# Bucketed attention with a rational feed-forward: the row maxima are clamped behind their transpose, and the bucket rows are scaled on ACT

## The chip, the cores and the metric

One core of a Trainium2 chip. Its engines are PE (TensorE: matmuls, with PEld, its weight loads, beside it), DVE (VectorE), ACT (ScalarE), POOL (GpSimd) and SP (SyncE, which issues most DMAs). Each engine works through its own queue in program order and waits on semaphores. The metric is the device time of one execution in microseconds (us); shorter is better.

## What is computed

Attention over 4 x 8 heads of 768 tokens and 64 dimensions, in which a query sees only the keys of its own hash bucket (6 bits, the signs of a projection), then a feed-forward layer whose activation is a quotient of polynomials:

```python
q_bits = (np.einsum('bhsd,dk->bhsk', q, proj) > 0).astype(np.int64)
...
mask = q_bucket[:, :, :, None] == k_bucket[:, :, None, :]
scores = scale * np.matmul(q, k.transpose(0, 1, 3, 2))
scores = np.where(mask, scores, -1000000000.0)
scores = scores - np.max(scores, axis=-1, keepdims=True)
attn = np.exp(scores)
attn = attn / (np.sum(attn, axis=-1, keepdims=True) + 1e-09)
out = np.matmul(attn, v)
...
P = a[0] + a[1] * h + a[2] * h2 + a[3] * h3          # h = x @ w_in
Q = 1.0 + np.abs(b[0]) * np.abs(h) + np.abs(b[1]) * h2
return (P / (Q + 1e-06)) @ w_out
```

## The kernel before

The heads are taken in 16 pairs (`p`), each in 12 steps (`s`): a step is one tile of 128 keys by 384 queries for both heads of the pair. What happens to a pair:

- `high`, `low`, `second_low`, `second_high`, `high_move` split q and k into a high and a low part and lay them out as matmul operands (Q1, K1, Q2, K2). The subtraction `low` writes a tile `lo` of which only one exists for q and one for k, so it waits until the DMAs of `second_low` have read the pair before.
- `bits` finds the bucket bits of two pairs at once (`psb`, 16 matmuls), turns them into signs on DVE, and scales the q rows by 2^60 (`mb`, a second DVE instruction). `maskrows` moves these rows by DMA into rows 64 to 76 of Q1 and K1, so that a matmul over 76 rows adds a huge negative number where the buckets differ.
- `maxstep` computes a 128-query strip of scores (`psm`, two buffers) and DVE reduces it to its row maximum, one column of `m`. Twelve such columns make a pair.
- `shift_clamp` clamps the maxima and changes their sign (`nm`, DVE, SBUF to SBUF). `shift_turn` transposes them on PE (`pst`, against the identity in `cst`) and copies the result out of PSUM (`mt`, ACT). `shift_rows` moves `mt` by DMA into row 76 of Q1: the scores then come out with the maximum taken off.
- `scores` computes the score tiles again (`pss`), ACT takes their exponential (`E`), and POOL adds the tiles up for the denominators (`acc`). `values` multiplies by v (`psv`). `pss` and `pst` share one PSUM tag of three buffers (`s`).

Pair p's `high`, `low`, `bits` and `maxstep` run during the two pairs before it, so in the steady state every step of a pair holds its own `scores` and `values` and a `maxstep` of the next pair or the one behind it. In between, `weights` converts the feed-forward weights, which arrive as 64-bit floats (`wr`, `ws`, `wi_lo`: some ACT and DVE instructions per block). Two pairs differ from two others only in that every second one holds a `bits`, and every fourth the reciprocals of a batch.

The order is written out by hand: `at(p, s, f, ...)` files a call under the number 12 p + s, and the plan is issued in the order of these numbers (equal ones in the order of filing). Every engine keeps this order. Pair 0 is special: its maxima come in two halves, each clamped, turned and stored by itself (`hf` 0 and 1), ahead of and during its own first steps.

The feed-forward part follows (`Ffn`: `psh`, `pso`), and shares no instruction with the functions named above.

Of the kernel before, what the change touches and what calls it, by code (L numbers as in the profile page):

```python
# [7 lines left out]
F32 = mybir.dt.float32  # L8
# [3 lines left out]
AF = mybir.ActivationFunctionType  # L12
ALU = mybir.AluOpType
# [4 lines left out]
P = 128  # L18
S = 768
HQ = 384  # L20
NT = S // P
# [13 lines left out]
CLAMP = 2.0 ** 40  # L35
# [30 lines left out]
def move(nc, out, in_, queue=None):  # L66

    (queue or nc.sync).dma_start(out.bitcast(F32), in_.bitcast(F32))
# [3 lines left out]
def bucket_attention_then_rational_ffn(ctx, tc, qT, kT, v, proj, w_in, w_out, coef, consts, out):  # L72
# [55 lines left out]
    def operands_to_terms():  # L128
        early.close()
        ffn.terms_pool(right)  # L130

    last = attention(tc, nc, raw, ps_b, tail, tokens, early, operands_to_terms, ffn, load, QF, KF, v, w_in, w_out, wo_d, ident, cst,
                     ones, prj, wi_hi, wi_lo, x_d, s_d, r_d, coefficients)
    ffn.rest(ctx, last)
# [3 lines left out]
def attention(ctx, tc, nc, raw, ps_b, tail, tokens, early, operands_to_terms, ffn, load, QF, KF, v, w_in, w_out, wo_d, ident, cst, ones, prj,  # L138
# [9 lines left out]
    sm = ctx.enter_context(tc.tile_pool(name="sm", bufs=1))  # L148
# [5 lines left out]
    Q1, Q2, K1, K2, LO, V, M, MB, ACC, EXP, AV, MS = ({} for _ in range(12))  # L154

    def load_v(p, queue=nc.sync):
        V[p] = operand("v", p, [P, NT, P], F32)
        queue.dma_start(V[p], v[p])
# [3 lines left out]
    def high(p, t):  # L162
        F, T, n = ((QF, Q1, "q"), (KF, K1, "k"))[t]
        T[p] = operand(f"{n}1", p, [P, 2, S], F32R, 3)
        nc.scalar.copy(T[p][:, t, :], F[p])

    def high_move(p):
        for T, g in ((Q1[p], 0), (K1[p], 1)):
            move(nc, T[0:64, 1 - g, :], T[64:128, g, :])

    def low(p, t, engine=nc.vector):
        F, T = ((QF, Q1), (KF, K1))[t]
        LO[p, t] = raw.tile([P, S], F32R, tag=f"lo{t}", name=f"lo{t}_{p}", bufs=1)
        engine.tensor_tensor(out=LO[p, t], in0=F[p], in1=T[p][:, t, :].bitcast(F32), op=ALU.subtract)
# [13 lines left out]
    def bits(p, which=(0, 1)):  # L188

        if which[0] == 0:  # L190
            mb = sm.tile([P, 2, HQ], F32R, tag="mb", name=f"mb{p}")
            MB[p], MB[p + 1] = (mb, 0), (mb, 64)
        mb = MB[p + which[0]][0]
        sl = slice(64 * which[0], 64 * which[-1] + 64)
        ps = ps_a.tile([P, 2, 512], F32, tag="psa", name=f"psb{p}_{which[0]}")
        for hf in range(2):
            for w in which:
                for t, F in enumerate((QF[p + w], KF[p + w])):
                    o = 64 * w + 32 * t
                    nc.tensor.matmul(ps[o : o + 32, hf, 0:HQ], prj[:, t, :], F[:, hf * HQ : hf * HQ + HQ], start=True, stop=True)  # L200
        rows = mb[sl]
        nc.vector.tensor_scalar(out=rows, in0=ps[sl, :, 0:HQ], scalar1=0.0, scalar2=cst[sl, 0:1], op0=ALU.is_gt, op1=ALU.subtract)
        nc.vector.tensor_scalar(out=rows, in0=rows.bitcast(F32), scalar1=cst[sl, 1:2], scalar2=None, op0=ALU.mult)

    def maskrows(p, queues=(None, None)):
        mb, o = MB.pop(p)
        for h in range(2):
            o1 = o + 14 * h
            move(nc, Q1[p][64:76, h, :], mb[o1 : o1 + 12].rearrange("p f c -> p (f c)"), queues[0])
            move(nc, K1[p][64:77, h, :], mb[o1 + 32 : o1 + 45].rearrange("p f c -> p (f c)"), queues[1])  # L210
# [9 lines left out]
        nc.vector.tensor_reduce(out=M[p][:, j : j + 1], in_=ps[:, :, 0:HQ], axis=AX.XY, op=ALU.max)  # L220


    def shift_clamp(p, hf=None):
        m = M[p].rearrange("p (h f i) -> p h f i", h=2, f=2)
        m = m if hf is None else m[:, :, hf : hf + 1, :]
        n = NT if hf is not None else 2 * NT
        MS[p] = sm.tile([P, n], F32, tag="nm", name=f"nm{p}_{hf}")
        nc.vector.tensor_scalar(out=MS[p].rearrange("p (h f i) -> p h f i", h=2, i=NT // 2), in0=m, scalar1=-CLAMP, scalar2=-1.0,
                                op0=ALU.max, op1=ALU.mult)

    def shift_turn(p, hf=None):
        n = NT if hf is not None else 2 * NT
        ps = ps_b.tile([P, 512], F32, tag="s", bufs=3, name=f"pst{p}_{hf}")
        nc.tensor.transpose(ps[0:n, 0:P], MS.pop(p), ident)
        MS[p] = sm.tile([n, P], F32R, tag="mt", name=f"mt{p}_{hf}")
        nc.scalar.copy(MS[p], ps[0:n, 0:P])

    def shift_rows(p, hf=None):
        cs = slice(0, S) if hf is None else slice(hf * HQ, hf * HQ + HQ)
# [62 lines left out]
    def recips(bb):  # L302
        n = 2 * NHP * S // P
        s = tail.tile([P, n], F32, tag="rs", name=f"rs{bb}")
        nc.sync.dma_start(s, s_d[bb].rearrange("h (x c) -> (h x) c", c=n))
        yield
        z = tail.tile([P, n], F32, tag="rz", name=f"rz{bb}")
        d = tail.tile([P, n], F32, tag="rd", name=f"rd{bb}")
        r = tail.tile([P, n], F32, tag="rr", name=f"rr{bb}")
        nc.vector.tensor_scalar(out=z, in0=s, scalar1=0.0, scalar2=S * TINY, op0=ALU.is_equal, op1=ALU.mult)  # L310
        nc.vector.tensor_scalar(out=d, in0=s, scalar1=0.0, scalar2=1e-9, op0=ALU.is_gt, op1=ALU.mult)
        nc.vector.tensor_tensor(out=d, in0=s, in1=d, op=ALU.add)
        nc.vector.tensor_tensor(out=d, in0=d, in1=z, op=ALU.add)
        nc.vector.reciprocal(out=r, in_=d)
        yield
        nc.sync.dma_start(r_d[bb].rearrange("h (x c) -> (h x) c", c=n), r)
        yield
# [43 lines left out]
    def at(p, s, f, *args):  # L361
        plan.setdefault(12 * p + s, []).append((f, args))

    def spread(p, steps, gen):
        for s in steps:
            at(p, s, lambda g: next(g, None), gen)

    for p in range(NPAIR):
        for s in range(12):
            at(p, s, scores, p, s)  # L370

            if p > 1:
                at(p - 2, 7 + s if p > 2 else 9 + 0.85 * s, maxstep, p, s)

            if not 0 < p < NPAIR - 1:
                at(p, s + 2.3, values, p, s)
            elif s % 2:
                at(p, s + 1.3, values, p, s - 1)
                at(p, s + 1.3, values, p, s)
            if s % NT == NT - 1:  # L380
                at(p, s + (1.3 if 0 < p < NPAIR - 1 else 2.3), values_out, p, s // NT)
        for hf in range(2):
            at(p, 6 * hf + 9, values_store, p, hf)
        if p < NPAIR - 1:
            at(p, 14.5, sums, p)
            at(p, 16, sums_store, p)
        if p > 1:
            for t in range(2):
                at(p - 2, t, high, p, t)
                at(p - 2, 2 + t, low, p, t)  # L390
            if p % 2 == 0:
                at(p - 2, 3 if p == 2 else 2, bits, p)
            at(p - 2, 2, high_move, p)
            at(p - 2, 6 if p == 2 else 4, maskrows, p)
        if p > 0:
            at(p - 1, 0, second_low, p)
            at(p - 1, 3, second_high, p)
            at(p - 1, 4, load_v, p)
            d = 1.5 if p == 1 else 0
            at(p - 1, 7 + d, shift_clamp, p)  # L400
            at(p - 1, 8 + d, shift_turn, p)
            at(p - 1, 10 if d == 0 else 9.6, shift_rows, p)
        if p > 3:
            at(p - 4, 6, load, p)
        if p % NHP == NHP - 1 and p + 1 < NPAIR:
            spread(p, (20, 22, 23), recips(p // NHP))
# [12 lines left out]
    for t in range(2):  # L419
        high(0, t)  # L420
        low(0, t)
    bits(0, (0,))
    high_move(0)
    maskrows(0, (nc.sync, nc.scalar))
    load(2, nc.scalar)
    load_v(0, nc.scalar)
    bits(0, (1,))
    for t in range(2):
        high(1, t)
    second_low(0)  # L430
# [5 lines left out]
        at(-2, when[s], maxstep, 0, order[s])  # L436
        at(0, 0.6 + 0.7 * s, maxstep, 1, s)
    for hf in range(2):
        for s, f in ((5, shift_clamp), (6.5, shift_turn), (6.6, shift_rows)):
            at(-2, 19.5 * hf + s, f, 0, hf)  # L440
    for t in range(2):
        low(1, t, nc.gpsimd)
# [211 lines left out]
```

## Time and profile before

| | |
|---|---|
| median of 3 runs | 1029.55 us (1029.2 to 1035.9) |
| the profiled execution | 1029.27 us, of which the span from first to last instruction is 1027.5 |
| PE busy | 977.0 us (95%), 5009 matmuls |
| DVE busy | 907.9 us (88%) |
| ACT busy | 678.9 us (66%) |
| POOL busy | 384.8 us (37%) |
| mean granted clock of PE | 0.971 |

All rows of a trace name line 61, since a helper records every operation; instructions are told apart by their tiles (`out<-in`). Busy time is the union of an engine's instructions; a matmul's end is modelled, so a busy PE need not be PE at its peak. In rows in order of time the columns are start, length (both us), engine, operation, tiles, and in brackets the idle time of the engine before it and what ended it; neighbours that are alike are merged (xN). In rows of waits they are total us, times, longest. Groups give busy us and the mean ns of one.

### The profile page before, as it was taken

The numbers are of one execution on the slowest core, as the hardware profiler recorded it, in microseconds if no ns is written. First come the engines' busy times: TensorE is split into PE (matmuls) and PEld (weight loads), VectorE is DVE, ScalarE is ACT, GpSimd is POOL, SyncE is SP. The second block draws the span as 40 slices with busy tenths as digits, with TensorE's granted clock in tenths as the row PEclk, the third lists the DMA queues.
The fourth block names the chain that finished last, engine by engine and source line by source line (L and its number), as shares of the span: only waits on it lengthen the run. The fifth ranks groups of instructions, "written<-read, shape, count | busy, mean of one in ns | idle before, by whom it ended". The sixth has DMA issues, their size and how long they took to land.

```text
span 1027.5 us, 14486 instructions
## 1 busy us (share of the span) xinstructions
PE 977.0 (95%) x5009; PEld 749.4 (73%) x5009; DVE 907.9 (88%) x1207; ACT 678.9 (66%) x1419; POOL 384.8 (37%) x268
## 2 busy tenths in 40 slices
PE   6899988989898988999999999999999999999998
PEld 2565555555555555564999999999999999999996
DVE  5688788878978787767999999999999999999996
ACT  1466555656656655567877777777777777777775
POOL 1255554545545454556222222222222222222222
PEclk7799999999999999899999999999999999999999
DMA  7765564656656664673740201101111010020000
GB/s 202 195 165 175 165 177 124 177 163 186 187 165 211 206 205 134 177 217 118 283 137 15 69 11 62 32 1 62 32 57 36 1 62 31 1 72 22 32 1 31
DMA packets 50489, 112.95 MB, mean 110 GB/s; under 512 B 9296, under 2 KB 21968, under 8 KB 50416
## 3 DMA queue, kind: packets, MB, share of 16 engines
q1 hardware_dynamic: 49580, 110.59, 35.8%
q10 hardware_dynamic: 836, 1.44, 0.5%
q8 instruction: 39, 0.64, 0.3%
q14 instruction: 34, 0.28, 0.1%
HBM read 56.82 MB, written 21.17 MB: 76 GB/s over the span
## 4 chain that ended last, share of the span: by engine, by line
PE 78%; DVE 13%; DMA 3%; issue 2%; ACT 2%; SPq 1%; DVEq 0%; ACTq 0%
PE psh L61 26%; PE pso L61 26%; PE psv L61 10%; PE pss L61 9%; PE psm L61 4%; DVE m L61 3%; DVE wr L61 2%; DVE ws L61 2%; DVE nm_None L61 2%; PE psu L61 2%; DVE wi_lo L61 2%; ACT E L61 1%; DMA k<-k 1%; PE psb L61 1%; SPq L61 1%
## 5 line engine op out<-in xcount | busy, mean ns | idle before, releaser
L61 POOL TENSOR_TENSOR gl<-c,gh 128x384 fp32r<-128x384 f32 x128 | 140.6, 1099 | 396.0 <-ACT gh L61 369.4
L61 DVE TENSOR_REDUCE m<-psm 128x1 f32<-128x768 f32 x192 | 180.1, 949 | 76.8 <-PE psm L61 76.2
L61 PE MATMUL pso<-wo,gh 128*128 128x512 f32 x768 | 241.1, 395 | 0.0
L61 ACT ACTIVATE E<-pss 128x384 f32<-128x384 f32 x384 | 168.4, 490 | 97.9 <-PE pss L61 92.4
L61 POOL TENSOR_TENSOR acc<-E,E 128x768 f32<-128x768 f32 x64 | 126.2, 1972 | 190.3 <-ACT E L61 190.3
L61 PE MATMUL pss<-q,k 77*128 77x384 f32 (+1 forms) x768 | 183.1, 361 | 3.0 <-DMA q<-mt 2.6
L61 PEld LDWEIGHTS pss<-q,k 77*128 77x128 f32 (+1 forms) x768 | 136.7, 196 | 64.6 <-issue 54.4
L61 PE MATMUL psh<-xl,wi_hi 128*128 128x384 f32 x512 | 172.1, 336 | 0.0
L61 PE MATMUL psh<-xh,wi_hi 128*128 128x384 f32 x512 | 171.7, 335 | 0.0
L61 PE MATMUL psh<-xh,wi_lo 128*128 128x384 f32 x512 | 171.5, 335 | 0.0
L61 PEld LDWEIGHTS pso<-wo,gh 128*128 128x128 f32 x768 | 142.9, 188 | 23.7
L61 PE MATMUL psv<-E,v 128*64 128x385 f32 x768 | 157.3, 529 | 0.0
L61 PE MATMUL pso<-wo,gl 128*128 128x512 f32 x384 | 152.2, 396 | 0.3 <-POOL gl L61 0.3
L61 DVE SCALAR_TENSOR_TENSOR c<-c,ab,r 128x384 f32<-128x384 f32 x128 | 147.1, 1149 | 0.0
L61 ACT ACTIVATE h<-psh 128x384 f32<-128x384 f32 x128 | 63.1, 493 | 122.4 <-PE psh L61 122.4
L61 POOL TENSOR_TENSOR acc<-acc,E 128x768 f32<-128x768 f32 x64 | 113.9, 1780 | 30.1 <-ACT E L61 27.5
L61 PE MATMUL psm<-k,q 76*128 76x384 f32 x384 | 111.1, 374 | 13.9 <-DVE m L61 9.8
L61 PEld LDWEIGHTS psh<-xh,wi_hi 128*128 128x128 f32 x512 | 96.1, 188 | 6.3 <-issue 1.2
L61 PEld LDWEIGHTS psh<-xl,wi_hi 128*128 128x128 f32 x512 | 96.0, 188 | 5.1
L61 PEld LDWEIGHTS psh<-xh,wi_lo 128*128 128x128 f32 x512 | 96.1, 188 | 0.0
L61 PEld LDWEIGHTS psm<-k,q 76*128 76x128 f32 x384 | 71.7, 204 | 31.8 <-DVE m L61 22.2
L61 PEld LDWEIGHTS psv<-E,v 128*64 128x64 f32 x768 | 47.6, 141 | 64.1 <-issue 56.7
(63 smaller groups left out, 1322.6 us busy)
## 6 DMA issues: line engine op xcount, KB each, us to landing
q<-q SPq DMA_DIRECT2D x48, 192.0 KB
k<-k SPq DMA_DIRECT2D x48, 192.0 KB
wr<-w_in SPq DMA_DIRECT2D x16, 512.0 KB
wr<-w_out SPq DMA_DIRECT2D x16, 512.0 KB
wo_d<-wr SPq DMA_DIRECT2D x16, 512.0 KB
wo<-wo_d SPq DMA_DIRECT2D x16, 512.0 KB
q<-lo SPq DMA_DIRECT2D x32, 192.0 KB
k<-lo SPq DMA_DIRECT2D x32, 192.0 KB
```

The source lines that it names most:

```text
L61: return self.tc.keep_in_program_order(issue(*args, **kwargs))
```

## The change

The maxima are transposed as they stand; the clamp and the change of sign happen on DVE when the result is read out of PSUM, where ACT copied it before. For the two halves of pair 0, whose columns are not adjacent, DVE first copies six columns into a tile. The scaling of the bucket rows becomes a function of its own, `penalties`, on ACT, filed one step behind `bits`.

```diff
-        rows = mb[sl]
-        nc.vector.tensor_scalar(out=rows, in0=ps[sl, :, 0:HQ], scalar1=0.0, scalar2=cst[sl, 0:1], op0=ALU.is_gt, op1=ALU.subtract)
-        nc.vector.tensor_scalar(out=rows, in0=rows.bitcast(F32), scalar1=cst[sl, 1:2], scalar2=None, op0=ALU.mult)
+        nc.vector.tensor_scalar(out=mb[sl], in0=ps[sl, :, 0:HQ], scalar1=0.0, scalar2=cst[sl, 0:1], op0=ALU.is_gt, op1=ALU.subtract)
+
+    def penalties(p, which=(0, 1)):
+        sl = slice(64 * which[0], 64 * which[-1] + 64)
+        rows = MB[p + which[0]][0][sl]
+        nc.scalar.activation(rows, rows.bitcast(F32), AF.Identity, scale=cst[sl, 1:2])
...
-    def shift_clamp(p, hf=None):
-        m = M[p].rearrange("p (h f i) -> p h f i", h=2, f=2)
-        m = m if hf is None else m[:, :, hf : hf + 1, :]
-        n = NT if hf is not None else 2 * NT
-        MS[p] = sm.tile([P, n], F32, tag="nm", name=f"nm{p}_{hf}")
-        nc.vector.tensor_scalar(out=MS[p].rearrange("p (h f i) -> p h f i", h=2, i=NT // 2), in0=m, scalar1=-CLAMP, scalar2=-1.0,
-                                op0=ALU.max, op1=ALU.mult)
-
     def shift_turn(p, hf=None):
-        n = NT if hf is not None else 2 * NT
+        n, m = 2 * NT, M[p]
+        if hf is not None:
+            n, m = NT, sm.tile([P, NT], F32, tag="nm", name=f"nm{p}_{hf}")
+            nc.vector.tensor_copy(m.rearrange("p (h i) -> p h i", h=2), M[p].rearrange("p (h f i) -> p h f i", h=2, f=2)[:, :, hf, :])
         ps = ps_b.tile([P, 512], F32, tag="s", bufs=3, name=f"pst{p}_{hf}")
-        nc.tensor.transpose(ps[0:n, 0:P], MS.pop(p), ident)
+        nc.tensor.transpose(ps[0:n, 0:P], m, ident)
         MS[p] = sm.tile([n, P], F32R, tag="mt", name=f"mt{p}_{hf}")
-        nc.scalar.copy(MS[p], ps[0:n, 0:P])
+        nc.vector.tensor_scalar(out=MS[p], in0=ps[0:n, 0:P], scalar1=-CLAMP, scalar2=-1.0, op0=ALU.max, op1=ALU.mult)
...
             if p % 2 == 0:
                 at(p - 2, 3 if p == 2 else 2, bits, p)
+                at(p - 2, 4 if p == 2 else 3, penalties, p)
...
-            at(p - 1, 7 + d, shift_clamp, p)
             at(p - 1, 8 + d, shift_turn, p)
...
     bits(0, (0,))
+    penalties(0, (0,))
...
     bits(0, (1,))
+    penalties(0, (1,))
...
-        for s, f in ((5, shift_clamp), (6.5, shift_turn), (6.6, shift_rows)):
+        for s, f in ((6.5, shift_turn), (6.6, shift_rows)):
             at(-2, 19.5 * hf + s, f, 0, hf)
```

DVE in the steady state, at the passage from pair 5's maxima (`m_1281` before, `m_1273` after) to those of pair 6. Before:

```order
L61 SCALAR_TENSOR_TENSOR ws_1408<-ws_1408,wr_1407 128x512
L61 TENSOR_REDUCE m_1281<-psm_11_1527 128x1
L61 ISA ws_1408<-wr_1407,ws_1408 128x1024
L61 TENSOR_SCALAR nm_None<-m_1281 128x12
L61 TENSOR_REDUCE m_1556<-psm_0_1557 128x1
L61 TENSOR_REDUCE m_1556<-psm_1_1580 128x1
```

And in the changed kernel:

```order
L61 SCALAR_TENSOR_TENSOR ws_1400<-ws_1400,wr_1399 128x512
L61 TENSOR_REDUCE m_1273<-psm_11_1519 128x1
L61 ISA ws_1400<-wr_1399,ws_1400 128x1024
L61 TENSOR_REDUCE m_1546<-psm_0_1547 128x1
L61 TENSOR_SCALAR mt_None<-pst_None 12x128
L61 TENSOR_REDUCE m_1546<-psm_1_1570 128x1
```

The clamp is gone from between the pair's last reduce and the next pair's first; an instruction that reads the transposed maxima stands one place further down.

PE at the same place in the changed kernel; before, the rows are the same but for the transpose, which read `nm_None` in place of `m_1273`:

```order
L61 MATMUL psm_0_1547<-k_6_1397,q_6_1372 128x384 x2
L61 MATMUL pss_8_0_1557<-q_4_838,k_4_863 128x384
L61 MATMUL pss_8_0_1557<-q_4_1105,k_4_1106 128x384
L61 MATMUL pss_8_1_1561<-q_4_838,k_4_863 128x384
L61 MATMUL pss_8_1_1561<-q_4_1105,k_4_1106 128x384
L61 MATMUL pst_None<-cst,m_1273 12x128
L61 MATMUL psm_1_1570<-k_6_1397,q_6_1372 128x384 x2
L61 MATMUL psv_1_1574<-E_148,v_1211 64x385 x2
```

PE's order is the same; the transpose needs the pair's last reduce alone.

DVE at the second half of pair 0's maxima (`m_215`; `m_298` and `m_296` are pair 1's, `lo_2` is pair 2's subtraction). Before:

```order
L61 TENSOR_REDUCE m_215<-psm_11_292 128x1
L61 TENSOR_SCALAR nm_1_296<-m_215 128x6
L61 TENSOR_REDUCE m_298<-psm_0_299 128x1
L61 TENSOR_REDUCE m_298<-psm_1_318 128x1
L61 TENSOR_TENSOR lo_2_331<-qf_182,q_2_290 128x768
L61 TENSOR_REDUCE m_298<-psm_2_335 128x1
L61 TENSOR_REDUCE m_298<-psm_3_348 128x1
```

And in the changed kernel:

```order
L61 TENSOR_REDUCE m_215<-psm_11_292 128x1
L61 TENSOR_REDUCE m_296<-psm_0_297 128x1
L61 TENSOR_REDUCE m_296<-psm_1_316 128x1
L61 TENSOR_TENSOR lo_2_329<-qf_182,q_2_290 128x768
L61 TENSOR_REDUCE m_296<-psm_2_333 128x1
L61 COPY nm_1_337<-m_215 128x6
L61 TENSOR_SCALAR mt_1_341<-pst_1_339 6x128
L61 TENSOR_REDUCE m_296<-psm_3_348 128x1
```

What the transpose of this half reads (`nm_1`) has moved from the place right behind the last reduce of pair 0 to one behind `lo_2` and pair 1's third reduce. On PE that transpose stands between `psm_2` and the first `psv` in both kernels.

ACT at the bucket rows of pairs 2 and 3 in the changed kernel:

```order
L61 ACTIVATE E_152<-pss_4_1_387 128x384
L61 ACTIVATE mb_366<-mb_366,cst 128x768
L61 ACTIVATE ws_314<-wr_313 128x512
L61 ACTIVATE wr_313<-wr_313 128x512
L61 ACTIVATE E_153<-pss_5_0_409 128x384
```

Before, the same rows stood there without the second one: the scaling now precedes the weights' two instructions.

## The prediction

> **What bounds the kernel now.** I read the stages first (busy time by stretch), since one average covers two different programs: the attention up to about 480 us, and the feed-forward part behind it.
>
> ```profile
> 600.00:700.00 100.00, 100.00 (x502) 90.32 (x501) 97.80 (x150) 75.16 (x153) 26.78 (x24) 1.00 0.09 31
> 108.40:136.90 28.50, 26.08 (x137) 16.15 (x137) 22.90 (x24) 17.15 (x38) 15.12 (x9) 0.94 0.56 161
> 310.90:339.50 28.60, 25.98 (x153) 16.01 (x154) 24.70 (x26) 17.15 (x38) 15.06 (x9) 1.00 0.73 224
> 368.00:398.10 30.10, 27.51 (x153) 16.61 (x153) 24.80 (x26) 17.17 (x38) 15.11 (x9) 0.95 0.65 192
> 427.70:455.00 27.30, 27.19 (x135) 17.25 (x135) 18.77 (x21) 14.75 (x34) 12.39 (x8) 0.87 0.64 190
> ```
>
> Columns: stretch, length, busy us of PE, PEld, DVE, ACT, POOL (with counts), granted clock, share of the DMA engines, GB/s. The feed-forward part is PE alone, 100.00 of 100.00, and the change touches nothing there. The other four rows each run from one transpose of the maxima to the next, one head pair per row. PE is busy about 26 of 28.6 us and DVE 22.9 to 24.8, so PE has a hole of 2 to 3 us per pair. Also, the granted clock is 0.94 or 0.95 in seven of the twelve such rows from 79.8 to 427.7, 1.00 in the other five, and 0.87 in the row behind them.
>
> The waits say what the hole is:
>
> ```profile
> PE pst_None L61 <- DVE nm_None L61: 23.4, 13, 1.9
> PE psm L61 <- DVE m L61: 9.8, 18, 0.8
> PEld pst_None L61 <- ACT E L61: 28.0, 15, 2.2
> L61 DVE TENSOR_SCALAR nm_None<-m x15: 160/1775/1779, 53.8 to 454.7; 128x12 f32<-128x12 f32 x15
> ```
>
> The transpose waited 13 times, 23.4 us in all, for a DVE clamp of 12 numbers per partition. That clamp takes 1775 ns in the median and 160 at best (min/median/max stand in the row). One case in order of time:
>
> ```profile
> 162.19 0.94 DVE L61 TENSOR_REDUCE m<-psm 128x1 f32<-128x768 f32 x1
> 163.66 1.78 DVE L61 TENSOR_SCALAR nm_None<-m 128x12 f32<-128x12 f32 x1
> 163.46 1.95 POOL L61 TENSOR_TENSOR acc<-E,E 128x768 f32<-128x768 f32 x1 [2.94 <-ACT E L61]
> 162.51 0.87 ACT L61 ACTIVATE E<-pss 128x384 f32<-128x384 f32 x2
> 164.29 0.87 ACT L61 ACTIVATE E<-pss 128x384 f32<-128x384 f32 x2
> 160.25 1.51 PE L61 MATMUL psv<-E,v 128*64 128x385 f32 x8
> 161.70 0.98 PE L61 MATMUL pss<-q,k 77*128 77x384 f32 x4
> 162.52 0.52 PE L61 MATMUL psm<-k,q 76*128 76x384 f32 x2
> 162.87 0.86 PE L61 MATMUL pss<-q,k 77*128 77x384 f32 x4
> 165.58 0.27 PE L61 MATMUL pst_None<-cst,nm_None 128*12 128x128 f32 x1 [1.85 <-DVE nm_None L61]
> 166.13 2.63 PE L61 MATMUL psv<-E,v 128*64 128x385 f32 x8
> 168.69 1.47 PE L61 MATMUL pss<-q,k 77*128 77x384 f32 x4
> ```
>
> The clamp starts while POOL's addition runs and ends at 165.44, 0.03 us behind it (163.46 + 1.95 = 165.41). POOL holds it up. PE is done at 163.73 and stands still to 165.58. Then the same matmuls run slower: 2.63 us for eight psv against 1.51 before, 1.47 for four pss against 0.98. So the clock fell behind the stall, and one stall cost 1.85 us and then 1.12 + 0.49 = 1.6 us.
>
> **The change, part by part.**
>
> *1. The clamp leaves the transpose's way: -23.4 us.* The transpose now reads the maxima. The last reduce that it needs ended at 162.19 + 0.94 = 163.13, 0.6 us before PE arrived, so no wait for DVE is left. Its other wait is for a buffer of the three shared with the scores. Two score tiles precede it in that step, so it takes the buffer of the step before, whose exponentials ended at 162.51 + 0.87 = 163.38, also in time. Behind it the next psm needs that same last reduce, and psv needs old exponentials: nothing is late. All of the 23.4 us go.
>
> *2. The clock stays up: -13.5 us.* Two rows of the same kind (153 matmuls) give the price: 30.10 us at clock 0.95 against 28.60 at 1.00, so 1.5 us per fall. Seven falls make 10.5; the row at 0.87 has a double one, 3.0. By the clock itself, (1 - clock) times length over the eight rows, it would be about 15.5. I take 13.5, and 15.5 as the far end.
>
> By the Trainium skill, page "TensorE: Matmul & The Clock Gate", Part 1 ("What's actually happening"), the gate falls to half speed after at least one idle window of about 3.4 us. By that rule a stall of 1.85 us would close nothing, and this term would be 0. The trace disagrees: the eight psv right behind the stall took 2.63 us.
>
> *3. The clamp out of PSUM on DVE, about 0.3 us for 15 pairs: 0.* This form is not in the trace. Bounds: 0.16 us (the clamp at its best) and 1.01 (768 elements out of PSUM, row below). By its 128 elements it is nearest to the short end: 0.16 + 128/768 x 0.85 = 0.30. It stands behind the next pair's first reduce, DVE saves 1.78 for it, and DVE's busy 23 to 25 us per pair fall by at least 0.8 even at the far bound. PE needs its buffer back two score steps later. ACT loses its copy of 0.25 us. Nothing is queued behind a wait that PE feels.
>
> *4. The bucket rows' scaling on ACT: +0.9 us, once.*
>
> ```profile
> L61 DVE TENSOR_SCALAR mb<-psb,cst x9: 1004/1006/1023, 8.9 to 383.4; 128x768 fp32r<-128x768 f32 x7, 64x768 fp32r<-64x768 f32 x2
> L61 DVE TENSOR_SCALAR mb<-mb,cst x9: 612/994/996, 9.9 to 384.4; 128x768 fp32r<-128x768 f32 x7, 64x768 fp32r<-64x768 f32 x2
> L61 ACT CAST q<-qf 128x768 fp32r<-128x768 f32 x16 | 13.3, 832 | 10.3 <-DMA k<-mb 8.1 <-DMA qf<-qT 2.2
> L61 ACT ACTIVATE xo<-psv,col 128x384 f32<-128x384 f32 x32 | 18.6, 582 | 1.0
> L61 ACT ACTIVATE E<-pss 128x384 f32<-128x384 f32 x384 | 168.4, 490 | 97.9 <-PE pss L61 92.4
> 155.65 0.79 SPq L61 DMA_DIRECT2D q<-mb  x1
> ```
>
> On ACT: 832 ns for the same tile as a cast, and 582 - 490 = 92 for an operand per partition: 0.92 us (bounds 0.83 and 1.02). DVE is rid of 0.99 in every second pair; PE waited there for reduces only 9.8 us in all, so I count no gain. ACT is busy 17 of 28 us, so 0.9 fits. SP issues the rows' DMAs at 155.65; ACT would have the rows at about 155.9, which delays them by 0.3 us, and the first psm that reads them is the one at 162.52. At the second pair it is tighter:
>
> ```profile
> 43.23 0.68 ACT L61 ACTIVATE ws<-wr 128x512 f32<-128x512 f32 x1
> 43.94 1.62 DVE L61 TENSOR_SCALAR wr<-wr 128x512 int32<-128x512 int32 x1 [0.54 <-ACT ws L61]
> ```
>
> DVE already waits 0.54 us for ACT's weights, the scaling now stands ahead of them, and that DVE instruction stands ahead of reduces: +0.9 (bounds 0 and 1.0). At the very start the rows are 0.3 us later (0.92 against 0.61 for 64 partitions), which the loads behind hide or not: +0.2.
>
> *5. The second half of pair 0: +4.1 us, and the clock +0.5.* Here the change moves work. The copy of six maxima now comes out at the transpose's place, behind two other DVE instructions.
>
> ```profile
> 31.04 0.17 DVE L61 TENSOR_SCALAR nm<-m 128x6 f32<-128x6 f32 x1
> 36.51 0.96 DVE L61 TENSOR_TENSOR lo<-qf,q 128x768 fp32r<-128x768 f32 x1 [2.84 <-DMA q<-mt]
> 37.39 1.82 DVE L61 TENSOR_REDUCE m<-psm 128x1 f32<-128x768 f32 x2
> 34.40 0.41 PE L61 MATMUL pst<-cst,nm 128*6 128x128 f32 x1
> 34.74 1.55 PE L61 MATMUL psv<-E,v 128*64 128x385 f32 x4
> 29.80:33.30 3.50, 3.50 (x12) 3.50 (x12) 2.57 (x4) 2.52 (x5) 0.66 (x1) 0.50 0.85 272
> 33.30:36.70 3.40, 3.40 (x11) 1.68 (x10) 0.56 (x2) 1.24 (x3) 2.85 (x2) 0.50 1.05 239
> 36.70:40.10 3.40, 3.40 (x18) 1.90 (x21) 3.37 (x4) 0.98 (x2) 0.00 (x0) 0.50 1.00 252
> ```
>
> The last three rows are stretches, with the columns as above. Before, the clamp was done at 31.21 and the transpose went at 34.40. Now DVE must first do the subtraction `lo`, which waits for a landing until 36.51, and a reduce (37.39 to 38.30); the copy takes 0.17 more, and PE can start the transpose at about 38.5: 4.1 us later, in a stretch where PE was busy throughout (3.40 of 3.40). Queued behind it are all of PE, SP's and ACT's DMA of the turned maxima and SP's moves for pair 1. The clock stood at 0.50 there and rose at 40.1, behind a stretch with bucket matmuls. It will rise one or two stretches of 3.4 us later: -0.35 or +1.35 us, taken as +0.5. The same move for the first half costs DVE some 0.8 us near 21, where PE next waits until 27.72 for a DMA; I take 0.
>
> *Sum.* -23.4 - 13.5 + 0.9 + 0.2 + 4.1 + 0.5 = -31.2 us on the profiled execution, which took 1029.27 us (span 1027.5 and 1.8 around it): **998.1 us**. The median of the runs, 1029.55, is 0.3 above; I say 998.
>
> **The rivals.**
>
> *The clock falls have another cause than the stalls.* Then term 2 is lost: 998 + 13.5 = 1011.5. For it stands that five of the thirteen stalls brought no fall. Against it: the slow psv begins at the stall's end. (The Trainium skill's rule on an idle window of 3.4 us, above, speaks for it.)
>
> *POOL holds up other DVE work.* The weights' instructions are stretched too, in some executions and not in others:
>
> ```profile
> L61 DVE SCALAR_TENSOR_TENSOR ws<-ws,wr x32: 672/1214/2167, 47.2 to 483.8; 128x512 int32<-128x512 int32 x32
> L61 DVE TENSOR_TENSOR wi_lo<-ws,wi_hi x16: 676/684/2334, 55.9 to 272.2; 128x512 fp32r<-128x512 f32 x16
> ```
>
> With pairs 3 us shorter they meet POOL's additions in other places. One more stretch of 2.33 - 0.68 = 1.65 us per pair, 13 times, is 21 us of DVE, of which PE may feel a third to two thirds (today's waits for reduces are 0.5 to 0.8 each): 998 + 7 to 14, about 1009. It can as well go the other way.
>
> *The transpose waits for ACT anyway.* The weight-load row above names ACT E, 28.0 us in 15 waits. If the wait is for the exponentials that end at 164.29 + 0.87 = 165.16, the change takes only 0.3 us from each of 13 stalls, the clock falls stay, and the prologue's 5.7 come on top: 1029.3 - 3.9 + 5.7 = 1031, no change. The buffer count in part 1 speaks against it.
>
> *Slower: the clock does not come back after the new stall at 34.6.* PE was busy 3.50 of 3.50 and 3.40 of 3.40 from 29.8 to 36.7 and still had 0.50; it rose only behind bucket matmuls. If only those open the gate, and the stall splits them over two stretches, PE works at half speed until the next ones:
>
> ```profile
> 91.94 0.51 PE L61 MATMUL psb<-qf,prj 128*32 128x384 f32 x1 [0.20 <-DVE m L61]
> ```
>
> That is 49 us of work taking 98: 998 + 47 = 1045. It decides against the change once more than 31 us of PE's work is done at half clock. Against it: behind the later falls the clock rose without bucket matmuls, as the 28.50 us row at 0.94 shows (3.4 us at half clock, no more). The same table of the skill's page says that one busy window of about 3.4 us opens the gate; by that rule this rival is out and the clock term is -0.35. The rows from 29.8 to 36.7 disagree with it.
>
> **How the numbers follow.** Forecast 0.75, stretched DVE work 0.09, clock falls stay 0.06, no change 0.05, slower 0.05. About 1% is what a measurement of this kernel can tell from no change, so 1019 and 1040 divide: faster 0.90, same 0.05, slower 0.05. Low end: the clock term at 15.5, a prologue of 3.5 in place of 5.7, and some 3 us of the 9.8 of reduce waits: 991. High end: the first rival, 1012; what lies above is left out.
>
> **What would show it.** Right: no wait of the transpose for DVE from 80 us on; pairs of 25 to 27 us with clock 1.00; the turned maxima written by DVE in about 0.3 us; a PE hole of about 4 us near 34.6 with `lo` ahead of the copy; the clock up at 43 to 47. Wrong: clock 0.94 without stalls, more waits of psm for reduces, or a hole that stays at the transpose.

## The result and the profile after

The changed kernel takes **989.8 us** (median; 989.2 to 991.7) against 1029.4 for the kernel before (1029.1 to 1035.9): ratio 0.960, 95% interval 0.956 to 0.964. The prediction was 998.0 with a range of 991 to 1012. The direction held, and so did the two large terms, the second within 2 us; 8.5 us of gain were missing from the sum, and the time came out just below the range.

Where the 39.7 us of span went (1027.5 to 987.8), by the starts of three matmuls in the two traces:

| stretch | before | after | difference |
|---|---|---|---|
| start to the transpose of pair 1's maxima | 55.53 | 60.17 | +4.6 |
| from there to the first feed-forward matmul (484.30; 444.65) | 428.8 | 384.5 | -44.3 |
| feed-forward part and end | 543.2 | 543.2 | 0 |

Stretches of the changed kernel, columns as in the prediction: two pairs in the steady state (the first without bucket bits, the second with), the stretch that had clock 0.87, and a piece of the feed-forward part.

```profile
109.38:134.31 24.93, 24.50 (x138) 15.68 (x137) 21.07 (x23) 16.81 (x37) 14.90 (x9) 1.00 0.67 190
134.31:160.11 25.80, 25.55 (x155) 16.14 (x154) 21.49 (x26) 17.56 (x38) 15.39 (x9) 1.00 0.67 190
391.31:415.38 24.07, 24.05 (x136) 15.38 (x136) 19.32 (x22) 15.61 (x36) 14.65 (x9) 1.00 0.77 218
600.00:700.00 100.00, 100.00 (x502) 90.33 (x502) 97.88 (x151) 75.05 (x151) 26.38 (x24) 1.00 0.10 32
```

But for the first and the last, a pair now takes 24.9 to 26.0 us in place of 28.5 to 30.1, PE is busy nearly throughout, and the clock is 1.00 everywhere behind the prologue. The waits of PE, with total us, times and longest:

```profile
PE psm L61 <- DVE m L61: 7.8, 15, 0.8
PE pst L61 <- DVE nm L61: 4.9, 2, 3.6
PE pst_None L61 <- DVE m L61: 0.2, 1, 0.2
```

The 23.4 us at `pst_None` have become 0.2; new are two waits in the prologue. One transpose of the steady state in order of time:

```profile
159.41 0.86 PE L61 MATMUL pss<-q,k 77*128 77x384 f32 x4
159.99 1.82 POOL L61 TENSOR_TENSOR acc<-E,E 128x768 f32<-128x768 f32 x1 [1.93 <-ACT E L61]
160.11 0.27 PE L61 MATMUL pst_None<-cst,m 128*12 128x128 f32 x1
160.66 1.51 PE L61 MATMUL psv<-E,v 128*64 128x385 f32 x8
160.88 0.27 DVE L61 TENSOR_SCALAR mt_None<-pst_None 12x128 fp32r<-12x128 f32 x1
```

PE runs through the transpose with no gap. The clamp out of PSUM takes 0.27 us while POOL's addition (159.99 to 161.81) is running: the clamp before, 128x12 from SBUF to SBUF, was held to the end of that addition; this one is not. The groups by form give both new instructions:

```profile
L61 DVE TENSOR_SCALAR mt_None<-pst_None 12x128 fp32r<-12x128 f32 x15 | 4.0, 270 | 0.5 <-PE pst_None L61 0.4
L61 ACT ACTIVATE mb<-mb,cst 128x768 fp32r<-128x768 f32 x7 | 6.6, 936 | 0.0
```

They were forecast at 300 and 920 ns.

### The profile page after: what moved, and what is told of

The parts are those of the page before. It is cut to its first block, busy times and chain, and to the rows that moved or that the text cites. A ratio compares the mean times of both kernels' runs of the same rounds, so it can differ in the third digit from the quotient of the medians.

```text
span 987.8 us, 14488 instructions
## 1 busy us (share of the span) xinstructions
PE 958.7 (97%) x5009; PEld 744.3 (75%) x5009; DVE 873.5 (88%) x1200; ACT 680.3 (69%) x1411; POOL 385.3 (39%) x268
## 4 chain that ended last, share of the span: by engine, by line
PE 87%; DVE 8%; issue 2%; DMA 2%; ACT 1%; SPq 0%; DVEq 0%; ACTq 0%
PE psh L61 27%; PE pso L61 27%; PE pss L61 12%; PE psv L61 12%; PE psm L61 6%; DVE m L61 3%; PE psu L61 2%; DVE ws L61 2%; PE psb L61 2%; DVE wr L61 1%; DVE wi_lo L61 1%; ACT E L61 1%; DMA q<-lo 1%; DVE c L61 0%; DMA prj<-proj 0%
## 5 line engine op out<-in xcount | busy, mean ns | idle before, releaser
L61 PE MATMUL pss<-q,k 77*128 77x384 f32 (+1 forms) x768 | 179.9, 357 | 2.6 <-DMA q<-mt 2.2
L61 PEld LDWEIGHTS pss<-q,k 77*128 77x128 f32 (+1 forms) x768 | 134.0, 192 | 60.1 <-issue 43.5
L61 PE MATMUL psv<-E,v 128*64 128x385 f32 x768 | 148.5, 503 | 0.0
L61 PE MATMUL psm<-k,q 76*128 76x384 f32 x384 | 107.6, 365 | 11.0 <-DVE m L61 7.8
```

What stands on the lines that cost most here:

```text
L61: return self.tc.keep_in_program_order(issue(*args, **kwargs))
```

## A reduce wait that vanished: reading the two traces

The term that the forecast lacked is visible at one place of every second pair, those with bucket bits. Before, with PE, DVE, POOL and ACT rows apart:

```profile
159.72 0.61 PE L61 MATMUL psm<-k,q 76*128 76x384 f32 x2 [0.57 <-DVE m L61]
156.47 2.33 DVE L61 TENSOR_TENSOR wi_lo<-ws,wi_hi 128x512 fp32r<-128x512 f32 x1
158.72 0.95 DVE L61 TENSOR_REDUCE m<-psm 128x1 f32<-128x768 f32 x1
156.02 2.22 POOL L61 TENSOR_TENSOR acc<-E,E 128x768 f32<-128x768 f32 x1 [3.61 <-ACT E L61]
154.09 1.86 ACT L61 ACTIVATE E<-pss 128x384 f32<-128x384 f32 x4
```

And the same place after:

```profile
153.84 0.68 DVE L61 TENSOR_TENSOR wi_lo<-ws,wi_hi 128x512 fp32r<-128x512 f32 x1
154.44 0.95 DVE L61 TENSOR_REDUCE m<-psm 128x1 f32<-128x768 f32 x1
153.99 2.24 POOL L61 TENSOR_TENSOR acc<-E,E 128x768 f32<-128x768 f32 x1 [4.22 <-ACT E L61]
151.46 0.87 ACT L61 ACTIVATE E<-pss 128x384 f32<-128x384 f32 x2
152.22 0.94 ACT L61 ACTIVATE mb<-mb,cst 128x768 fp32r<-128x768 f32 x1
153.04 0.87 ACT L61 ACTIVATE E<-pss 128x384 f32<-128x384 f32 x2
```

Before, POOL's addition starts 0.45 us ahead of `wi_lo`, which then takes 2.33 us and makes the reduce late, and PE waits 0.57 us. After, ACT's scaling stands between two pairs of exponentials, the second pair comes later, POOL waits 4.22 us in place of 3.61, and `wi_lo` gets in 0.15 us ahead of it and takes 0.68. Two things changed at once here, though: ACT got 0.94 us of work, and DVE lost 0.99.

My theory after this reading, **POOL phase**: the delay on ACT is what counts. The rivals: **DVE relief** (the missing 0.99 us lets the reduces come in time), and **clamp** (the missing 1.78 us does).

## The experiments

**1. The transposed clamp alone** (scaling back on DVE):

```diff
-    def penalties(p, which=(0, 1)):
...
+        nc.vector.tensor_scalar(out=mb[sl], in0=mb[sl].bitcast(F32), scalar1=cst[sl, 1:2], scalar2=None, op0=ALU.mult)
...
-                at(p - 2, 4 if p == 2 else 3, penalties, p)
...
```

> The changed kernel with the bucket rows' scaling back on DVE, right behind the instruction that makes the signs; the maxima are still clamped out of PSUM. Three theories on the reduce waits that went (about 0.55 us, with 0.1 us of restart, in each of the seven pairs that hold a bits): POOL phase (the scaling on ACT delays exponentials and so POOL's addition by 0.6 us, and the DVE subtraction wi_lo, which starts at the same time, escapes it): wi_lo is back at 2.33 us in the pairs with bits, the 0.55 us waits are back, +4.5 us, less about 1.0 of the prologue: 993.3. DVE relief (0.99 us less work): the waits are back too, 993.3, whatever wi_lo does. Clamp (its 1.78 us gone from DVE): waits stay away, 988.8. All: no transpose waits for DVE, clock 1.00 from 46 us on.

Measured 994.5 us (994.0 to 995.4), ratio 0.966 (0.964 to 0.968). The waits of PE for reduces and the place shown above:

```profile
PE psm L61 <- DVE m L61: 10.1, 19, 0.8
154.14 2.32 DVE L61 TENSOR_TENSOR wi_lo<-ws,wi_hi 128x512 fp32r<-128x512 f32 x1
153.70 2.22 POOL L61 TENSOR_TENSOR acc<-E,E 128x768 f32<-128x768 f32 x1 [3.64 <-ACT E L61]
```

`wi_lo` is back at 2.32 us and the waits are back. The clamp theory is out; the other two agree with this. From the transpose of pair 1's maxima to the first feed-forward matmul this run took 390.1 us against 384.5 of the changed kernel: the moved scaling is worth 5.6 us there. Its clock column reads 1.00 throughout, even at 32.57 us, where four `pss` take 1.48 us, so it says nothing here; the matmuls do: from 46 to 419 us four `pss` in a row take 0.86 to 0.99 us, but for one group that holds a wait. So there is no fall of the clock in that stretch, and of the 428.8 before, 38.7 us belong to the clamp's move.

**2. The same, and ACT gets an idle load** where the changed kernel scales, so that DVE has its whole work and ACT is as late as after the change:

```diff
+    def act_load(p):
+        spare = sm.tile([P, HQ], F32, tag="spare", name=f"spare{p}")
+        for hf in range(2):
+            nc.scalar.activation(spare, KF[p][:, hf * HQ : hf * HQ + HQ], AF.Identity, scale=cst[:, 1:2])
...
+                at(p - 2, 4 if p == 2 else 3, act_load, p)
...
```

> As the first kernel (scaling on DVE, 0.99 us), and ACT gets an idle load of the same length at the step at which the changed kernel scales: two activations of 128x384 into a spare tile. POOL phase: wi_lo at 0.68 us in the pairs with bits and no reduce wait there, although DVE has its full load: within 1 us of the changed kernel, 989 to 990.5. DVE relief: the waits of 0.55 us stay as in the first kernel: 993 to 994.

Measured 989.8 us (988.4 to 992.9), ratio 0.962 (0.959 to 0.964): as the changed kernel, 4.7 us faster than the first experiment by nothing but useless work on ACT. The waits for reduces over the whole execution, and the place shown above:

```profile
PE psm L61 <- DVE m L61: 7.5, 14, 0.8
152.37 0.99 DVE L61 TENSOR_SCALAR mb<-mb,cst 128x768 fp32r<-128x768 f32 x1
157.02 0.68 DVE L61 TENSOR_TENSOR wi_lo<-ws,wi_hi 128x512 fp32r<-128x512 f32 x1
157.49 1.93 POOL L61 TENSOR_TENSOR acc<-E,E 128x768 f32<-128x768 f32 x1 [4.54 <-ACT E L61]
155.39 1.27 ACT L61 ACTIVATE spare<-kf,cst 128x384 f32<-128x384 f32 x2
```

DVE does its scaling (152.37) and `wi_lo` takes 0.68 us all the same. From 60 us on, PE's waits for reduces are 5.6 us as in the changed kernel, against 8.9 in experiment 1, and a pair with bits takes 25.8 to 25.9 us as there. DVE relief is out; POOL phase stands.

**3. The scaling on ACT alone**, in the kernel before:

```diff
-        nc.vector.tensor_scalar(out=rows, in0=rows.bitcast(F32), scalar1=cst[sl, 1:2], scalar2=None, op0=ALU.mult)
+    def penalties(p, which=(0, 1)):
+        sl = slice(64 * which[0], 64 * which[-1] + 64)
+        rows = MB[p + which[0]][0][sl]
+        nc.scalar.activation(rows, rows.bitcast(F32), AF.Identity, scale=cst[sl, 1:2])
...
+                at(p - 2, 4 if p == 2 else 3, penalties, p)
...
```

> The kernel before with only the bucket rows' scaling moved to ACT; the clamp stays ahead of the transpose. POOL phase or DVE relief: seven reduce waits of about 0.55 us and their restarts go (-4.6), the prologue pays 1.1: 1026, with the 13 stalls of 1.85 us still there. Clamp: 1030.5. The clock falls may come in other pairs, since a pair of pairs is then 57.5 us and not 58.1 (17.0 windows of 3.41): each fall more or less is 1.6 to 1.7 us, so 1018 to 1031.

Measured 1006.4 us (1004.4 to 1007.8), ratio 0.977 (0.974 to 0.980): 20 us below the 1026 of POOL phase and DVE relief, and 12 below the expected range. **4. The kernel before with the idle load on ACT and nothing else** is the sharper form of it (the two added blocks of experiment 2, on the kernel before):

> The kernel before, nothing moved and nothing removed; ACT alone gets an idle load of 0.9 us (two activations of 128x384 into a spare tile) in every second pair, at the step at which the changed kernel scales. POOL phase: POOL's additions come 0.6 us later there, wi_lo and in these pairs the clamp too escape them, and six or seven stalls go with some clock falls, as in the run that moved the scaling alone: 1004 to 1009. DVE relief: DVE has as much to do as before, so nothing is gained: 1028 to 1031.

Measured 1010.8 us (1006.4 to 1012.0), ratio 0.981 (0.978 to 0.985). Work was only added, and the kernel is 18 us faster: from the transpose of pair 1's maxima to the first feed-forward matmul PE stands still for 19.8 us in place of 34.4. Its waits, its clamps, and one clamp with the addition beside it:

```profile
PE pst_None L61 <- DVE nm_None L61: 12.3, 7, 1.9
L61 DVE TENSOR_SCALAR nm_None<-m x15: 159/903/1778, 54.4 to 437.4; 128x12 f32<-128x12 f32 x15
162.28 0.16 DVE L61 TENSOR_SCALAR nm_None<-m 128x12 f32<-128x12 f32 x1
162.27 1.84 POOL L61 TENSOR_TENSOR acc<-E,E 128x768 f32<-128x768 f32 x1 [1.94 <-ACT E L61]
```

Seven stalls are left of thirteen. In the pairs with bits DVE, no longer held at `wi_lo`, comes to the clamp within 0.05 us of POOL's start on its addition, and the clamp takes 0.16 us in all six. My expectation for experiment 3 had missed this: it followed the freed `wi_lo` to the reduce behind it and not to the clamp, seven instructions behind `wi_lo`.

**5. The stall alone**: the kernel before with the transposes (pair 1's excepted) one step later.

```diff
-            at(p - 1, 8 + d, shift_turn, p)
+            at(p - 1, 9 if d == 0 else 9.5, shift_turn, p)
```

> The kernel before with every later pair's transpose filed one step (2.2 us) later and nothing else: the clamp stays on DVE, stretched to 1.78 us, but PE has a step of other work while it runs. If the stall in front of the transpose is what costs the 23 us, and the clock falls follow from it: no wait of the transpose for DVE, clock 1.00 from 46 us on, waits of psm for reduces as before: 1029.2 - 23.2 - 15.5 = 990.5. If the clock falls have another cause: 1006. If the clamp's time on DVE matters by itself: above 995 with clock 1.00.

Measured 992.5 us (991.6 to 993.4), ratio 0.964 (0.961 to 0.967).

```profile
L61 DVE TENSOR_SCALAR nm_None<-m x15: 163/1792/1803, 53.6 to 418.6; 128x12 f32<-128x12 f32 x15
134.77 0.27 PE L61 MATMUL pst_None<-cst,nm_None 128*12 128x128 f32 x1
134.77:161.51 26.74, 25.92 (x154) 15.97 (x153) 23.80 (x25) 17.01 (x39) 14.12 (x8) 1.00 0.64 182
161.51:187.68 26.17, 24.79 (x139) 15.56 (x137) 23.89 (x30) 17.00 (x39) 15.17 (x9) 1.00 0.61 176
```

The clamps are as stretched as ever (1792 ns in the median), no transpose waits, and the clock is 1.00 behind the prologue. So the stall in PE's way is the cost, and the clock falls come from the stalls: 36 us for one edited line. The time is 2.0 us above the 990.5 expected: from the transpose of pair 1's maxima to the first feed-forward matmul this run took 393.0 us, against 390.1 in experiment 1. Whether these 3 us are the clamp's time on DVE or the transpose's new place is not separated here.

**6. The prologue**: the changed kernel with the copy of pair 0's six maxima filed where the clamp had been.

```diff
+    def half_copy(p, hf):
+        m = MS[p, hf] = sm.tile([P, NT], F32, tag="nm", name=f"nm{p}_{hf}")
+        nc.vector.tensor_copy(m.rearrange("p (h i) -> p h i", h=2), M[p].rearrange("p (h f i) -> p h f i", h=2, f=2)[:, :, hf, :])
...
-        for s, f in ((6.5, shift_turn), (6.6, shift_rows)):
+        for s, f in ((5, half_copy), (6.5, shift_turn), (6.6, shift_rows)):
```

> The changed kernel with the copy of six maxima of pair 0's halves filed where the clamp was (right behind the last reduce), the rest as it is. Theory of the prologue: PE's hole of 3.6 us before the second half's transpose goes, the clock rises one or two windows of 3.4 us earlier or not: 986 (985 to 987). Rival: what is late behind it (lo at 36 to 37 and the reduce behind it) holds PE up in its place: 988.5 to 990.

Measured 986.0 us (984.7 to 986.9), ratio 0.958 (0.955 to 0.960), 3.9 below the changed kernel. The changed kernel's prologue first (DVE, PE), then this one's:

```profile
35.98 1.04 DVE L61 TENSOR_TENSOR lo<-qf,q 128x768 fp32r<-128x768 f32 x1 [2.40 <-DMA q<-lo]
36.94 0.94 DVE L61 TENSOR_REDUCE m<-psm 128x1 f32<-128x768 f32 x1
37.81 0.15 DVE L61 COPY nm<-m 128x6 f32<-128x6 f32 x1
38.11 0.37 PE L61 MATMUL pst<-cst,nm 128*6 128x128 f32 x1 [3.61 <-DVE nm L61]
```

```profile
30.52 0.17 DVE L61 COPY nm<-m 128x6 f32<-128x6 f32 x1
34.17 0.41 PE L61 MATMUL pst<-cst,nm 128*6 128x128 f32 x1
```

The hole of 3.61 us ended behind `lo`, a reduce and the copy, in the order that the prediction gave, and goes with the early copy. The clock rose earlier too, at 35.7 us in place of 45.2, and the transpose of pair 1's maxima came at 54.43 in place of 60.17. In this trace 0.9 us of these 5.7 were lost again behind it.

**7. The rest of the reduce waits**: the changed kernel with `wi_lo` of every second block moved ahead of a reduce and of `lo`; **8.** the same with the early copy.

```diff
+        if i % 2 and i < 2 * NFC - 1:
+            late = (10.5, 11.9, 13.5, 14.5)
         spread(0, [o + x for x in (4, 7, 8, 9) + late], weights(i))
```

> The changed kernel with every second weight block's last subtraction (wi_lo, and its like for w_out) filed 0.6 of a step earlier, ahead of a reduce and of lo, when POOL is idle. If its stretching by POOL is what makes the remaining reduce waits of 0.55 us in the pairs without bits: it takes 0.68 us everywhere, these waits go with their restart, 0.8 us for each of six pairs: 985. If the waits have another cause, or the reduce behind it is late in its place: 989 to 991.

> The changed kernel with the early copy of pair 0's maxima and the earlier wi_lo together. If the two are independent: 985.95 - 4.8 = 981. If the earlier wi_lo brings nothing: 986.

Measured 986.2 us (984.9 to 987.9), ratio 0.958 (0.955 to 0.961), and with both **981.8 us** (981.0 to 983.8), ratio 0.954 (0.951 to 0.957), the fastest version here. The first one's waits and a `wi_lo` of a pair without bits, with POOL beside it:

```profile
PE psm L61 <- DVE m L61: 4.5, 10, 0.8
174.06 2.17 DVE L61 TENSOR_TENSOR wi_lo<-ws,wi_hi 128x512 fp32r<-128x512 f32 x1
173.54 2.14 POOL L61 TENSOR_TENSOR acc<-acc,E 128x768 f32<-128x768 f32 x1 [0.25 <-ACT E L61]
176.28 0.96 DVE L61 TENSOR_REDUCE m<-psm 128x1 f32<-128x768 f32 x1
```

The time came within 1.2 us of the 985 expected, the reason only in half: `wi_lo` still meets an addition of POOL (another one, 173.54) and takes 2.17 us. But it now does so where DVE otherwise stood idle for 2.15 us waiting for the next `psm`, and no reduce is late behind it.

## Why the prediction was wrong, point by point

| term | forecast | measured | from |
|---|---|---|---|
| 1. stalls of the transpose | -23.4 | -23.2 | waits 23.4 to 0.2 |
| 2. clock falls | -13.5 | -15.5 | remainder: 38.7 of experiment 1, less 23.2 |
| 3. clamp out of PSUM | 0 | 0 | 0.27 us, no wait behind it |
| 4. scaling on ACT, steady state | 0 | -5.6 | 390.1 to 384.5 |
| 4, 5. prologue | +5.7 | +4.6 | 55.53 to 60.17 |
| sum | -31.2 | -39.7 | |

**The step that failed is in part 4**: "DVE is rid of 0.99 in every second pair; PE waited there for reduces only 9.8 us in all, so I count no gain." It priced the removed DVE instruction by its own length and the added ACT instruction by ACT's free time. Neither is what it did. In each of the six pairs with bits behind the prologue it moved POOL's addition by some 0.6 us against DVE, past the start of `wi_lo`. Each time 1.65 us of stretching went, and with it 0.57 of waiting and what PE loses behind a wait: from one transpose to the next such a pair took 26.6 to 27.2 us in the first experiment and 25.8 to 25.9 in the changed kernel. The row was on the table: the rival of POOL's additions quoted `wi_lo` at 676 to 2334 ns, and ended with "It can as well go the other way". But it was priced on the slow side only, and tied to the pairs' new length. What would have settled it was to lay the ACT row in front of the exponentials that POOL waits for: before, `wi_lo` starts 0.45 us behind POOL, and 0.94 us of ACT work stands ahead of what POOL waits for.

**Term 2 was undersized, by 2 us or less.** The price per fall, 1.5, came from two rows with equal matmul counts, but the slow one held only 3.2 us at half clock (368.0 to 371.2), not a whole window of 3.4. The 15.5 measured is a remainder, which also holds what PE loses behind a stall besides the clock; the far end named beside the forecast, 15.5 by the clock itself, agrees with it. Experiment 5 has no falls either and saved 35.7 us in the same stretch (428.8 to 393.0). Less 23.4 of stalls that leaves 12.3, but PE stood still there for 12.7 us in other places, against 11.0 in experiment 1.

**Parts 1, 3 and 5 held.** The stalls went whole, nothing was late behind the transpose, and the hole came with `lo` ahead of the copy. It was 3.6 us in place of 4.1, since `lo` got its landing at 35.98 and not at 36.51. What is left of the 4.6, 1.0 us for the start, the later clock and the later weights against 1.6 forecast, can't be split further: the first transpose came at 21.04 before and at 21.26 after, but at 20.4 and 20.5 in experiments 5 and 4, whose work up to there is that of the kernel before. The clock was up at 45.2, within the 43 to 47 forecast.

**The rivals.** That the falls have another cause is refuted by experiment 5, where they went with the stalls. That the transpose waits for ACT anyway is refuted by the trace. The slower case had as its mechanism that only bucket matmuls open the clock; in the run with the scaling alone the clock rose ahead of them (first ones of pair 2 at 38.22). Its sum, besides, adds 47 us where 49 us of work taking 98 adds 49. The rows:

```profile
32.20:35.60 3.40, 3.40 (x13) 2.20 (x11) 0.96 (x1) 2.23 (x5) 2.89 (x2) 0.50 1.04 277
35.60:38.20 2.60, 1.62 (x8) 1.01 (x6) 1.86 (x3) 0.87 (x2) 0.61 (x1) 1.00 1.01 265
```

The low end of the range took 3 us of reduce waits, the far clock term and a prologue of 3.5 together and still stopped at 991: it counted 3 us where the moved scaling brought 5.6.

## What to carry to other kernels

Where one engine's instruction takes 0.68 us in some executions and 2.33 in others, its cost may be, as here, a matter of which engine starts first. A change that moves either by half a microsecond must then be priced for that, on both sides: lay the rows of all three engines at that place side by side and see what stands ahead of the one that starts first. An edit that only adds work can then gain (18 us here), so the sign of a term cannot be read from the work it adds. And before the work of a stalled producer is redesigned, try its consumer one step later: one line of the order brought 36 us, where the whole change, which lost 4.6 in the prologue, brought 39.6.

## What the runs showed of the hardware that I had not expected

A clamp with its source in PSUM took 0.27 us during an addition of POOL, where the one from SBUF to SBUF took 1.78; and that one got through too (0.16 us) when it started within 0.01 us of the addition. The Trainium skill, page "SBUF — State Buffer", section "SBUF: two separate sides", says that the port pair which DVE and POOL share is an exclusive lock: a DVE instruction with two inputs in SBUF (or in a mode that uses both ports) and one of POOL that reads SBUF get it by who starts first, for the whole instruction. The rows of `wi_lo`, which has two such inputs, agree: 2.33 us when POOL was 0.45 ahead, 0.68 when it was 0.15 behind. I had read POOL's effect as a slowdown of work that overlaps it, and not as a race for the start.

Of PE's clock: the kernel before and the run with the scaling alone show holes with and without a fall behind them. Two stretches of the first, each with the stretch behind it, then one of the second:

```profile
163.00:166.40 3.40, 1.55 (x10) 0.95 (x10) 3.40 (x5) 2.02 (x5) 2.86 (x2) 1.00 0.46 169
166.40:169.80 3.40, 3.40 (x11) 1.60 (x8) 0.79 (x1) 0.01 (x1) 0.77 (x1) 0.50 0.03 9
193.70:197.10 3.40, 1.91 (x11) 0.82 (x11) 3.10 (x3) 1.32 (x4) 3.00 (x2) 1.00 0.57 202
197.10:200.50 3.40, 3.40 (x20) 2.56 (x20) 1.96 (x3) 2.48 (x6) 0.65 (x1) 1.00 0.01 2
76.50:80.00 3.50, 2.20 (x12) 1.53 (x13) 3.47 (x6) 2.20 (x6) 2.79 (x2) 0.99 0.87 289
80.00:83.40 3.40, 3.40 (x12) 1.65 (x9) 0.76 (x1) 0.06 (x1) 0.71 (x1) 0.50 0.05 17
```

The falls of one run lie whole multiples of 3.41 us apart (58.0, 27.3 and 30.7 us in the kernel before). Behind a window of that grid in which PE stood still for 1.85 us the clock fell (166.4), behind one with 1.49 (3.40 less 1.91) it did not (197.1). This fits that up to 340 us every second stall of equal length brought a fall: from one transpose to the next but one it was 57.1 to 58.5 us, about 17 windows (58.0), so the same stall met nearly the same place of the grid each time. The last four stalls each brought one. But a plain share of time is not the rule: in the trace of experiment 4 PE stood still for the same 1.49 us from 405.30 to 408.70 and the clock fell, and in the third case above 1.3 us brought a fall at 80.0. In experiment 4 the stall lay at the window's end, in the kernel before at its start; whether that decides is not shown. Nor is the rise in the prologue explained: with PE fully busy it came at 35.6 to 46.6 us in the runs, in some behind two full windows, in the kernel before behind three. Both stay open. (By the Trainium skill, page "TensorE: Matmul & The Clock Gate", Part 1, section "What's actually happening", the window is free-running and 3413 ns long, with which the spacing of the falls agrees; its idle window of that whole length is not what a fall needs here, since 1.85 us of standing still was enough.)
